# A dilated gated convolution: loads of the projection weights and of two input chunks wait until the transpose of oct 4 has landed

## Chip, cores, metric

The kernel runs on one core of a Trainium2 chip. The metric is the device time of one execution in microseconds (us); a profiled execution also gives the span from its first to its last instruction.

## The reference

A causal convolution with 15 taps and dilation 2 over x (2 x 16000 x 144, bfloat16) into 288 channels, a gate, and a projection:

```
xp = jnp.pad(x, ((0, 0), (pad, 0), (0, 0)))          # pad = 28
h = sum over i of xp[:, pad - 2*i : pad - 2*i + T, :] @ w[i]   # w: 15 x 144 x 288
z = tanh(h[..., :144]) * sigmoid(h[..., 144:])
return z @ w_o                                        # w_o: 144 x 144
```

(The sum is written here in one line; the reference loops over i.)

## The kernel before

The 32000 time steps are cut into 128 stretches of 250, one for each partition. Step e of all stretches is a tile of 128 rows; eight steps in succession are an *oct*, numbered -4 to 30, the negative ones holding the steps that the taps reach back to. TensorE needs each tile transposed (channels on partitions). Of the 144 channels, 128 go by one way and 16 by another:

- Input chunks of 16 steps (two octs) are loaded by SP's queue into `Xr` (two slots, line 500). Chunk 0 has octs 1 and 2, chunk 1 octs 3 and 4, chunk 2 octs 5 and 6, chunk 3 octs 7 and 8.
- `load_xa(o)` (line 653) copies 128 channels of an oct to `STA`, on ScalarE for octs 1 to 4 and on VectorE later, and SP issues a transposing DMA from `STA` to `XA`.
- The last 16 channels are gathered in `XBc` (lines 545, 546), differenced (646), copied to `STB` (680), and SP issues a transposing DMA to `XB` (684).
- Octs up to 0 are transposed by TensorE in the prologue (579).

The convolution is a fast algorithm: VectorE forms differences of the transposed tiles (`V`, `DU`, `DD`, `GX`, `GU`, `GV`, `GD`, line 700) and sums of the weights (630), so that a unit needs 64 matmuls (all through line 747). A pair of octs is worked in two *units* u; there are 30. A unit's items carry the names S0, S1, VE, VF, X0a to X1b, Y0a, Y0b, Y01 and D00 to D11. Among them ScalarE copies PSUM banks (905, 932, 974) and VectorE adds them: line 1026 writes into memory that was `Xp`, 1038 and 1047 add in PSUM. A D item ends four results: ScalarE takes tanh (768) and sigmoid (771), VectorE multiplies into `Z` (776). SP transposes `Z` into `ZT` (829, "ship"), TensorE multiplies by the projection weights `WOR` (846), ScalarE evicts (854), SP stores (865). Projections are the O items: up to three groups an oct of 4, 4 and 3 matmuls. The first group that is due is that of oct -1, in step 1.

`WOR` holds sixteen shifted pieces of w_o and is loaded by sixteen DMAs from GpSimd (line 1189). Every projection reads all of it.

**Order of work.** Two things set it. `PATTERNS` gives, for a step t (default `PATTERN`), the order of items in TensorE's main stream; a name with "+" belongs to unit t + 1, one without to unit t, and an item whose unit does not exist, or an O whose group is not yet due, is left out. Between them, preparation of later octs is put in, tied to the matmul it follows by `soft`. Then a planner (`_Graph.schedule`, line 113) simulates the five engines and one DMA resource with durations written in the code, and fixes from that the order of instructions on every engine and queue, and the PSUM banks. TensorE's main items keep their given order; prologue matmuls are `floating` and fill holes. On the chip each engine runs its list in order and waits on semaphores only for true dependencies (`deps`). So a new dependency acts twice: as a wait on the chip, and through a new plan.

The loads that the change touches hang on `xb2`, the transposing DMA of oct 2's `XB`: WOR's sixteen (line 1191) and the chunks from 2 on (line 1198); chunk 1 hangs on the last weight load.

Of the kernel before, what the change touches and what calls it, by code (L numbers as in the profile page):

```python
# [327 lines left out]
def _conv_wavenet_kernel(nc, x, w, w_o, out):  # L328
    B, T, D = x.shape
# [37 lines left out]
    KF = 0  # L367
    WARMS = 0
    LAG = 2
    PATTERNS = {29: 'O2 O1 Y01 Y0a D11 O0 Y0b D01 D00 D10', 28: 'Y0a X0a+ O1+ Y0b X0b+ O2+ D11 S0+ D10 X1a+ D00 Y01 S1+ X1b+ VE+ O0+ D01 VF+', 1: 'X0a+ Y0a O1+ O2+ Y0b X0b+ D11 X1a+ D00 S0+ O0+ X1b+ Y01 S1+ D10 D01 VE+ VF+', 0: 'Y0a X0a+ Y0b X0b+ D11 D00 S0+ D10 O2+ O1+ Y01 S1+ X1a+ D01 VE+ X1b+ VF+ O0+', 2: 'Y0a O0+ X0a+ O1+ Y0b X0b+ D11 D00 X1a+ S0+ D10 Y01 S1+ X1b+ D01 VE+ VF+ O2+', -1: 'X0a+ Y0a Y01 O2+ Y0b S0+ D11 D10 X0b+ O1+ X1a+ S1+ X1b+ D01 VE+ D00 O0+ VF+', 27: 'Y0a O2+ X0a+ O1+ Y0b X0b+ D11 D00 S0+ X1a+ D10 Y01 S1+ X1b+ D01 VE+ O0+ VF+'}  # L370
    AACT = (1, 2, 3, 4)
    BDVE = (3, 4)
    EARLYC = 0
# [6 lines left out]
    with contextlib.ExitStack() as st:  # L380
        def sb(name, shape, dt):
            return st.enter_context(nc.sbuf_tensor(name, shape, dt))
# [4 lines left out]
        STA = sb("STA", [NP, NST, 8, 128], BF16)  # L387
        STB = sb("STB", [NP, NST, 12, 128], BF16)
        XA = sb("XA", [NP, NA, 8, 128], BF16)
# [12 lines left out]
        WOR = sb("WOR", [NP, 16, D], BF16)  # L402
# [14 lines left out]
        x_t, w_t, wo_t, out_t = x.tensor, w.tensor, w_o.tensor, out.tensor  # L417

        g = _Graph()
# [25 lines left out]
        def aslot(o):  # L445
            return (o + 4) % NA
# [7 lines left out]
        def bslot(o):  # L454
            return (o + 1) % NB
# [20 lines left out]
        def ld_x(tile_ap, p0, p1, e0, e1):  # L476
            def f(e):
                src = bass.AP(x_t, (p0 * L - H + e0) * D, [[L * D, p1 - p0], [1, (e1 - e0) * D]])
                return e.dma_start(tile_ap, src)
            return f  # L480

        def flat(ap):
            return ap.rearrange("p e d -> p (e d)")
# [13 lines left out]
        def load_xchunk(ci):  # L497
            a, c = CH[ci]
            s = ci % NX
            return g.add("sp", ld_x(flat(Xr[:, s, 0:c - a, :]), 0, NP, E0 + a, E0 + c), w=[("Xr", s)], dur=0.5, dma="xr", nbytes=NP * (c - a) * D * 2)  # L500
# [18 lines left out]
        wa_op = wa_ops[LOADS[-1][1]] if LOADS[-1][0] == "w" else wa_ops[0]  # L519
# [50 lines left out]
        for pi in range(4):  # L570
            e0, e1 = pro_pieces[pi]
            for o in range(-4, 1):
# [3 lines left out]
                b = 6 + o % 2  # L576
# [35 lines left out]
        for o, tiles, bb in ((-1, range(E0 - 4, E0), 7), (0, range(E0, E0 + 8), 6)):  # L612
            fns = []
            for e in tiles:
# [6 lines left out]
                  r=[bk], w=[("XB", bslot(o))], frees=[bk], dur=0.5 if o < 0 else 0.92)  # L621
# [11 lines left out]
        def chunk_of(t):  # L633
            return [ci for ci, (a, c) in enumerate(CH) if a <= t < c][0]
# [6 lines left out]
        def diff_b(eng, m0, nm, r, tag):  # L641
            i0 = MB - m0 - nm

            def f(v):
                pat = lambda ph, grp: bass.AP(XBc[:].tensor, (ph * MB + i0) * DB, [[8 * MB * DB, NP], [grp, 2], [MB * DB, 2], [1, nm * DB]])
                return v.tensor_tensor(pat(2, -2 * MB * DB), pat(6, -2 * MB * DB), pat(4, 2 * MB * DB + DB), ALU.subtract)
            g.add(eng, f, r=r, w=[tag], dur=t_tt(4 * nm * DB), prio=2 if gate else 0, soft=gate[:1])

        def diff_chunk(ci):
            a, c = CH[ci]  # L650
            diff_b("dve", (E0 + a + 2) // 4, (c - a) // 4, [("XBc", ci), ("XBc", ci - 1)] if ci else [("XBc", 0)] + hk5, ("XBd", ci))

        def load_xa(o):
            s, q = aslot(o), o % NST
            ci = chunk_of(8 * o)
            i0 = 8 * o - CH[ci][0]
            src = Xr[:, ci % NX, i0:i0 + 8, 0:DA]
            if o in AACT:
                g.add("act", lambda a: a.activation(STA[:, q, :, :], src, ACT.Copy), r=[("Xr", ci % NX)], w=[("STA", q)], dur=0.92, prio=1, soft=gate[:1])  # L659
            else:  # L660
                g.add("dve", lambda v: v.tensor_copy(STA[:, q, :, :], src), r=[("Xr", ci % NX)], w=[("STA", q)], dur=0.335, prio=2, soft=gate[:1])
            g.add("sp", lambda e: e.dma_start_transpose(XA[:, s, :, :], STA[:, q, :, :].rearrange("p a b -> p (a b)")),
                  r=[("STA", q)], w=[("XA", s)], dur=1.3, dma="xa", nbytes=8 * 128 * 128 * 2)

        def load_xb(o, parts=(0, 1)):
            s, q = bslot(o), o % NST
            e0 = E0 + 8 * o
            ck = set()
            for e in range(e0 - 28, e0 + 8):
                if e >= EP:  # L670
                    ck.update([("XBc", chunk_of(e - E0)), ("XBd", chunk_of(e - E0))])
                else:
                    ck.update(hk5 + ["XBcz", "XBd_h"])
            m4 = (e0 + 2) // 4

            for h in parts:
                def cp(v, h=h):
                    src = bass.AP(XBc[:].tensor, (MB - 1 - m4 - h) * DB, [[8 * MB * DB, NP], [MB * DB, 6], [1, 128]])
                    dst = STB[:, q, 6 * h:6 * h + 6, :]
                    return v.tensor_copy(dst, src) if o in BDVE else v.activation(dst, src, ACT.Copy)  # L680
                g.add("dve" if o in BDVE else "act", cp, r=sorted(ck, key=str), w=[("STB", q, h)], dur=0.27 if o in BDVE else 0.708, prio=2 if gate else 0, soft=gate[:1])
            if 1 not in parts:
                return
            return g.add("sp", lambda e: e.dma_start_transpose(XB[:, s, :, :], STB[:, q, :, :].rearrange("p a b -> p (a b)")),
                  r=[("STB", q, 0), ("STB", q, 1)], w=[("XB", s)], dur=1.7, dma="xb", nbytes=12 * 128 * 128 * 2)
# [44 lines left out]
        def g_diffs(m, only=None):  # L730
            o0, o1, q = 2 * m + 1, 2 * m + 2, gslot(m)
            for src, sn, sl, n, dst, key, kk in ((XA, 8, aslot, 2, GX, "GX", lambda o: [("XA", aslot(o))]),
                                                 (DU, 4, uslot, 4, GU, "GU", lambda o: [("DU", uslot(o))]),
                                                 (V, 8, vslot, 2, GV, "GV", lambda o: [("V", vslot(o), 0)]),
                                                 (DD, 8, uslot, 6, GD, "GD", lambda o: [("DD", uslot(o))])):
                if only is not None and key not in only:
                    continue
                a1, am, c = sl(o1) * sn, sl(o0 - 1) * sn, sl(o0) * sn
                if n < 6:
                    tt(ap(dst, q * 2 * n, [(n, 2), n]), ap(src, a1, [(am - a1, 2), n]), ap(src, c, [(0, 2), n]),  # L740
                       kk(o1) + kk(o0) + kk(o0 - 1), [(key, q, 0), (key, q, 1)], 2 * n * TR)
                    continue
                for d, a0, ox in ((0, a1, o1), (1, am, o0 - 1)):
                    tt(ap(dst, (q * 2 + d) * n, [n]), ap(src, a0, [n]), ap(src, c, [n]), kk(ox) + kk(o0), [(key, q, d)], n * TR)
# [417 lines left out]
        xb2 = load_xb(2)  # L1162
# [19 lines left out]
        for o in range(-2, 1):  # L1182
            v_third(o)
        g_diffs(-1)
        for dl in range(8):
            for part in range(2):
                r0, r1, s0 = (16 * dl, 128, 0) if part == 0 else (0, 16 + 16 * dl, 128 - 16 * dl)
                def f(e, r0_=r0, r1_=r1, s0_=s0, i_=2 * dl + part):
                    return e.dma_start(WOR[r0_:r1_, i_, :], bass.AP(wo_t, s0_ * D, [[D, r1_ - r0_], [1, D]]))
                op = g.add("pool", f, r=["WORz"], w=[("WORp", dl, part)], dur=0.5, dma="wor", nbytes=(r1 - r0) * D * 2)  # L1190
                op.deps.add(xb2)

        nl = [1]
        nd = [1]

        def fetch(o):
            while nl[0] < len(CH) and CH[nl[0]][0] <= 8 * o:
                load_xchunk(nl[0]).deps.add(wa_op if nl[0] < 2 else xb2)
                nl[0] += 1

        def prep(o):
# [17 lines left out]
        def prepare(m):  # L1219
            o0, o1 = 2 * m + 1, 2 * m + 2  # L1220
            if m >= NPAIR:
                return []
            return [lambda: v_first(o0), lambda: v_second(o0), lambda: v_first(o1), lambda: v_second(o1), lambda: g_diffs(m, ("GX",)),
                    lambda: g_diffs(m, ("GU",)), lambda: v_third(o0), lambda: v_third(o1), lambda: g_diffs(m, ("GV",)),
                    lambda: g_diffs(m, ("GD",))]
# [7 lines left out]
        def pattern_of(t):  # L1233
            return [(x.rstrip("+"), x.count("+")) for x in PATTERNS.get(t, PATTERN).split()]

# [5 lines left out]
        for f in stage(1):  # L1241
            f()
        gate[:] = []
        for f in prepare(0):
            f()
        todo_p = []
        for t in range(-reach, NUN):
# [3 lines left out]
            for name, off in pattern_of(t):  # L1251
# [20 lines left out]
                if name[0] == "D":  # L1272
                    done_d[u] = done_d.get(u, 0) + 1
                    m, r, o0, o1 = octs(u)
# [12 lines left out]
        m, r, o0, o1 = octs(NUN - 1)  # L1287
# [89 lines left out]
```

## Time and profile before

| | us |
|---|---|
| median of 8 runs | 321.55 (320.85 to 322.27) |
| profiled execution | 321.6 |
| its span | 319.6 |
| TensorE busy | 311.9 (98%) |
| VectorE busy | 284.4 (89%) |
| ScalarE busy | 267.4 (84%) |
| granted TensorE clock | 0.997 |

In the profile's rows PE is TensorE's matmuls, PEld its weight loads, DVE VectorE, ACT ScalarE, POOL GpSimd, SP the queue that issues most DMAs ("q" marks a sequencer). A row of the timeline or of the chain begins with its start and its length in us; `xN` merges N instructions; `<-` names the tile written and those read, or in brackets what ended the wait ahead of it. A matmul's length includes its way through the array; successive ones start 0.123 us apart. A row of stretches gives the busy time of PE, PEld, DVE, ACT and POOL, the granted clock, the share of the sixteen DMA engines (over 1 where packets overlap) and GB/s. In a row of DMA issues the last number is the time from issue to landing.

### The profile page before, as it was taken

To read this page: it belongs to the slowest core of one execution; us is meant where nothing else is said; L and a number is where in the kernel's file an instruction comes from. 1 tells how busy PE (TensorE), PEld (TensorE's weight loads), DVE (VectorE), ACT (ScalarE), POOL (GpSimd) and SP (SyncE) were. 2 spreads that over 40 slices of the span, in tenths; PEclk is the share of its full clock that TensorE was granted. 3 is DMA by queue.
4 is the path that set the end of the run, shared out by engine and by line. 5 is a ranking of instruction groups with operands and counts; after the bars stand their busy time and mean duration, and the time that the engine had idled before them with its cause. 6 is when DMAs were issued, how large, how long until landed. Compare 5 with 4: busy or idle time off the path is not lost.

```text
span 319.6 us, 6912 instructions
## 1 busy us (share of the span) xinstructions
PE 311.9 (98%) x2643; PEld 239.9 (75%) x2643; DVE 284.4 (89%) x615; ACT 267.4 (84%) x635; POOL 17.0 (5%) x29
## 2 busy tenths in 40 slices
PE   7999999999999999999999999999999999999994
PEld 7677667777777777777777777777777777777674
DVE  1999999999999998998989999898989989894774
ACT  3796699899897988979798897979889797788774
POOL 8105400000000000000000000000000000000000
PEclk9999999999999999999999999999999999999998
DMA  8699959959888493979949695895949477131553
GB/s 201 206 197 173 258 108 226 171 144 178 192 159 215 93 246 83 207 157 131 251 78 238 106 201 154 146 198 121 227 118 178 104 127 188 44 71 74 113 129 94
DMA packets 127821, 50.38 MB, mean 158 GB/s; under 512 B 119134, under 2 KB 121615, under 8 KB 127789
## 3 DMA queue, kind: packets, MB, share of 16 engines
q1 hardware_dynamic: 127273, 49.62, 75.1%
q0 software_dynamic: 512, 0.33, 0.5%
q8 instruction: 20, 0.33, 0.4%
q14 instruction: 12, 0.10, 0.1%
q10 hardware_dynamic: 4, 0.01, 0.0%
HBM read 11.82 MB, written 9.22 MB: 66 GB/s over the span
## 4 chain that ended last, share of the span: by engine, by line
PE 89%; ACT 6%; DMA 2%; DVE 1%; issue 1%; POOL 0%; ACTq 0%; POOLq 0%
PE PS L747 77%; PE PS L846 9%; DMA XA<-STA 2%; ACT STB L680 2%; PE PS L554 1%; ACT STA L659 1%; PE PS L579 1%; ACT XA L588 1%; ACT XB L620 0%; ACT TS L768 0%; ACT TS L771 0%; PE PS L552 0%; PE PS L877 0%; ACT PS L905 0%; PE PS L804 0%
## 5 line engine op out<-in xcount | busy, mean ns | idle before, releaser
L1026 DVE TENSOR_TENSOR Xp<-PS,UX 128x576 f32<-128x576 f32 x90 | 63.0, 750 | 16.8 <-PE PS L747 16.6
L747 PE MATMUL PS<-WB,XB 128*128 128x288 bf16 x260 | 72.1, 286 | 0.0
L747 PE MATMUL PS<-WA,GD 128*128 128x288 bf16 x360 | 70.0, 286 | 0.1
L1038 DVE TENSOR_TENSOR PS<-PS,Xp 128x576 f32<-128x576 f32 x90 | 68.2, 758 | 2.1 <-ACT OS L854 1.0
L768 ACT ACTIVATE TS<-PS 128x288 f16<-128x288 f32 x125 | 51.7, 413 | 13.2 <-PE PS L747 12.2
L854 ACT ACTIVATE OS<-PS 128x432 bf16<-128x432 f32 (+1 forms) x88 | 42.4, 489 | 13.9 <-PE PS L846 12.8
L771 ACT ACTIVATE TS<-PS 128x288 f16<-128x288 f32 x125 | 51.4, 411 | 0.0
L905 ACT ACTIVATE PS<-PS 128x288 f32<-128x288 f32 x120 | 46.3, 408 | 2.8 <-PE PS L747 2.8
L974 ACT ACTIVATE UX<-PS 128x576 f32<-128x576 f32 x60 | 39.2, 654 | 10.7 <-PE PS L747 10.4
L680 ACT ACTIVATE STB<-XBc 128x768 bf16<-128x768 bf16 x56 | 47.5, 855 | 0.0
L747 PE MATMUL PS<-WS,GU 128*128 128x288 bf16 x210 | 44.3, 287 | 0.0
L846 PE MATMUL PS<-WOR,ZT 128*128 128x144 bf16 (+1 forms) x322 | 42.4, 253 | 0.3 <-DVE Xp L1026 0.3
L747 PEld LDWEIGHTS PS<-WA,GD 128*128 128x128 bf16 x360 | 33.7, 98 | 11.3 <-DVE PS L1038 3.1
L776 DVE TENSOR_TENSOR Z<-TS 128x288 bf16<-128x288 f16 x125 | 36.6, 298 | 4.4 <-ACT TS L771 4.2
L747 PE MATMUL PS<-WC,XB 128*128 128x288 bf16 x120 | 34.3, 286 | 0.0
L846 PEld LDWEIGHTS PS<-WOR,ZT 128*128 128x128 bf16 x322 | 27.9, 98 | 6.6 <-DVE Xp L1026 0.5
L747 PE MATMUL PS<-WD,DD 128*128 128x288 bf16 x180 | 31.9, 286 | 0.2 <-ACT PS L905 0.2
L747 PE MATMUL PS<-WC,V 128*128 128x288 bf16 x180 | 30.6, 286 | 0.0
L747 PE MATMUL PS<-WA,DD 128*128 128x288 bf16 x180 | 30.6, 286 | 0.0
L747 PEld LDWEIGHTS PS<-WB,XB 128*128 128x128 bf16 x260 | 25.4, 98 | 6.7 <-ACT XB L620 0.3
L747 PE MATMUL PS<-WA,V 128*128 128x288 bf16 x118 | 25.7, 286 | 0.3 <-ACT PS L1111 0.3
L747 PE MATMUL PS<-WT,DU 128*128 128x288 bf16 x120 | 24.5, 286 | 0.0
(93 smaller groups left out, 460.5 us busy)
## 6 DMA issues: line engine op xcount, KB each, us to landing
Xr<-in_x_dram SPq DMA_DIRECT2D x15, 576.0 KB, 4.6
out_dram<-OS SPq DMA_DIRECT2D x30, 288.0 KB, 3.1
WA<-in_w_dram SPq DMA_DIRECT2D x3, 288.0 KB, 5.8
ZT<-Z SPq DMA_TRANSPOSE x32, 3.7
Xp<-in_x_dram SPq DMA_DIRECT2D x2, 252.0 KB, 5.9
XA<-STA SPq DMA_TRANSPOSE x30, 3.5
XB<-STB SPq DMA_TRANSPOSE x30, 4.5
Xp<-in_x_dram SPq DMA_DIRECT2D x1, 441.0 KB, 4.6
```

Of the source, the lines that this page charges most:

```text
L554: fns += [lambda t: t.matmul(PS[:, BANK_O * 512:BANK_O * 512 + 128], lhsT=ID[:], rhs=ONES[:], start=True, stop=True)] * max(0, n - 12)
L680: return v.tensor_copy(dst, src) if o in BDVE else v.activation(dst, src, ACT.Copy)
L747: return lambda t: t.matmul(bank(bk.b), lhsT=lhs(), rhs=rhs(), start=start, stop=True, skip_group_check=True)
L768: return a.activation(TS[:, s, 0, :, :], both(bk, 0, D), ACT.Tanh)
L771: return a.activation(TS[:, s, 1, :, :], both(bk, D, D), ACT.Sigmoid)
L776: return v.tensor_tensor(dst, TS[:, s, 0, :, :], TS[:, s, 1, :, :], ALU.mult)
L846: return t.matmul(PS[:, c0:c0 + n * D], lhsT=ZT[:, zt, blk, :], rhs=WOR[:, wi:wi + n, :].rearrange("p a b -> p (a b)"), start=first, stop= ...
L854: return e.tensor_copy(dst, src) if eng == "dve" else e.activation(dst, src, ACT.Copy)
L905: g.add("act", lambda e: e.activation(bank(bk.b + 1), bank(bk.b), ACT.Copy), w=[bk], dur=t_act(N2), prio=0)
L974: g.add("act", lambda e: e.activation(UX[:, k, u % NU, :, :], both(X, 0, N2), ACT.Copy), r=[X], w=[("UX", k, u % NU)], frees=[X], dur=t_ac ...
L1026: g.add("dve", lambda v, k=k, wi=wi, vb=vb, us=us: v.tensor_tensor(wslot(wi), both(vb, 0, N2), UX[:, k, us, :, :], ALU.add), r=[vb, ("UX", ...
L1038: return v.tensor_tensor(both(d, 0, N2), src, wslot(wi), ALU.add)
```

## The change

Three edits. WOR's sixteen loads are added to the program later, after the staging of octs 3 and 4, and depend on the transposing DMA of oct 4 into `XA` instead of `xb2`. Chunk loads from chunk 2 on depend on that DMA too (chunks behind 3 are loaded far later anyway). The patterns of steps -1, 0, 1, 2, 28 and 29 are new, and step 3, which had the default, has one of its own; every pattern holds the same items as before.

```diff
-    PATTERNS = {29: 'O2 O1 Y01 Y0a D11 O0 Y0b D01 D00 D10', 28: 'Y0a X0a+ O1+ Y0b X0b+ O2+ D11 S0+ D10 X1a+ D00 Y01 S1+ X1b+ VE+ O0+ D01 VF+', 1: 'X0a+ Y0a O1+ O2+ Y0b X0b+ D11 X1a+ D00 S0+ O0+ X1b+ Y01 S1+ D10 D01 VE+ VF+', 0: 'Y0a X0a+ Y0b X0b+ D11 D00 S0+ D10 O2+ O1+ Y01 S1+ X1a+ D01 VE+ X1b+ VF+ O0+', 2: 'Y0a O0+ X0a+ O1+ Y0b X0b+ D11 D00 X1a+ S0+ D10 Y01 S1+ X1b+ D01 VE+ VF+ O2+', -1: 'X0a+ Y0a Y01 O2+ Y0b S0+ D11 D10 X0b+ O1+ X1a+ S1+ X1b+ D01 VE+ D00 O0+ VF+', 27: 'Y0a O2+ X0a+ O1+ Y0b X0b+ D11 D00 S0+ X1a+ D10 Y01 S1+ X1b+ D01 VE+ O0+ VF+'}
+    PATTERNS = {29: 'O1 O0 O2 Y0a D11 Y01 Y0b D01 D00 D10', 28: 'Y0a X0a+ O0+ Y0b X0b+ D11 S0+ O1+ D00 D10 X1a+ Y01 S1+ X1b+ VE+ D01 O2+ VF+', 1: 'X0a+ Y0a X0b+ Y0b D11 O0+ O2+ D00 X1a+ S0+ Y01 X1b+ S1+ D10 D01 VE+ VF+ O1+', 0: 'Y0a X0a+ O2+ Y0b X0b+ O1+ D11 S0+ D00 D10 S1+ X1a+ O0+ Y01 VE+ X1b+ D01 VF+', 2: 'O1+ Y0a X0a+ O0+ Y0b X0b+ D11 D00 X1a+ S0+ D10 Y01 S1+ X1b+ D01 VE+ VF+ O2+', -1: 'Y0a Y0b O2+ Y01 D10 D11 X0a+ S0+ O0+ X0b+ X1a+ S1+ D00 O1+ D01 X1b+ VE+ VF+', 27: 'Y0a O2+ X0a+ O1+ Y0b X0b+ D11 D00 S0+ X1a+ D10 Y01 S1+ X1b+ D01 VE+ O0+ VF+', 3: 'Y0a X0a+ O2+ O1+ Y0b D11 X0b+ D00 S0+ X1a+ D10 Y01 S1+ X1b+ D01 VE+ VF+ O0+'}
...
+        land = {}
+
         def load_xa(o):
...
-            g.add("sp", lambda e: e.dma_start_transpose(XA[:, s, :, :], STA[:, q, :, :].rearrange("p a b -> p (a b)")),
+            land[o] = g.add("sp", lambda e: e.dma_start_transpose(XA[:, s, :, :], STA[:, q, :, :].rearrange("p a b -> p (a b)")),
...
-        for dl in range(8):
-            for part in range(2):
...
-                op = g.add("pool", f, r=["WORz"], w=[("WORp", dl, part)], dur=0.5, dma="wor", nbytes=(r1 - r0) * D * 2)
-                op.deps.add(xb2)
-
...
-                load_xchunk(nl[0]).deps.add(wa_op if nl[0] < 2 else xb2)
+                load_xchunk(nl[0]).deps.add(wa_op if nl[0] < 2 else land.get(4, xb2))
...
         for f in stage(1):
             f()
         gate[:] = []
+        for dl in range(8):
+            for part in range(2):
...
+                op = g.add("pool", f, r=["WORz"], w=[("WORp", dl, part)], dur=0.5, dma="wor", nbytes=(r1 - r0) * D * 2)
+                op.deps.add(land[4])
+
```

More of the change, by code (lines that the diff above doesn't have):

```diff
@@ L1184, in _conv_wavenet_kernel @@
         g_diffs(-1)
-        for dl in range(8):
-            for part in range(2):
-                r0, r1, s0 = (16 * dl, 128, 0) if part == 0 else (0, 16 + 16 * dl, 128 - 16 * dl)
-                def f(e, r0_=r0, r1_=r1, s0_=s0, i_=2 * dl + part):
-                    return e.dma_start(WOR[r0_:r1_, i_, :], bass.AP(wo_t, s0_ * D, [[D, r1_ - r0_], [1, D]]))
-                op = g.add("pool", f, r=["WORz"], w=[("WORp", dl, part)], dur=0.5, dma="wor", nbytes=(r1 - r0) * D * 2)
-                op.deps.add(xb2)
         nl = [1]
@@ L1243, in _conv_wavenet_kernel, with f @@
         gate[:] = []
+        for dl in range(8):
+            for part in range(2):
+                r0, r1, s0 = (16 * dl, 128, 0) if part == 0 else (0, 16 + 16 * dl, 128 - 16 * dl)
+                def f(e, r0_=r0, r1_=r1, s0_=s0, i_=2 * dl + part):
+                    return e.dma_start(WOR[r0_:r1_, i_, :], bass.AP(wo_t, s0_ * D, [[D, r1_ - r0_], [1, D]]))
+                op = g.add("pool", f, r=["WORz"], w=[("WORp", dl, part)], dur=0.5, dma="wor", nbytes=(r1 - r0) * D * 2)
+                op.deps.add(land[4])
         for f in prepare(0):
```

## The prediction

> **What bounds the kernel now.** I read the page's first and fourth parts first: which engine is busy, and what the chain that ended last consists of.
>
> ```profile
> PE 311.9 (98%) x2643; PEld 239.9 (75%) x2643; DVE 284.4 (89%) x615; ACT 267.4 (84%) x635; POOL 17.0 (5%) x29
> PE 89%; ACT 6%; DMA 2%; DVE 1%; issue 1%; POOL 0%; ACTq 0%; POOLq 0%
> ```
>
> TensorE sets the time; the other 11% lies at the two ends. The chain in order of time says where:
>
> ```profile
> 28.64 5.93 DMA XA<-STA
> 34.60 0.76 DVE V L700 x2
> 35.36 0.69 DVE PS L1038
> 36.09 2.68 PE PS L747 x20
> ...
> 62.83 7.89 PE PS L747 x64
> ```
>
> From 53 us on a unit is 64 convolution matmuls in 7.9 us (0.123 us each) with eleven projection matmuls after them, and nothing can be taken out there by moving loads. The transpose of oct 4 (issued 28.64, landed 34.57) is the only DMA in the chain after 28 us. Next I asked what stands around it: the transposes and loads on SP, WOR's sixteen loads on GpSimd, and landing times.
>
> ```profile
> 27.09 1.51 SPq L684 DMA_TRANSPOSE XB<-STB  x1
> 28.64 1.83 SPq L662 DMA_TRANSPOSE XA<-STA  x1
> 30.51 2.76 SPq L684 DMA_TRANSPOSE XB<-STB  x1
> 33.32 1.06 SPq L479 DMA_DIRECT2D Xr<-in_x_dram  x2
> ```
> ```profile
> 27.42 8.50 POOL L1189 DMA_DIRECT2D WOR<-in_w_o_dram  x16 [14.57 <-DMA XB<-STB]
> ```
> ```profile
> XA<-STA SPq DMA_TRANSPOSE x30, 3.5
> DMA to landing us min/median/max: 4.0/4.6/5.8
> WOR<-in_w_o_dram POOLq DMA_DIRECT2D x1, 36.0 KB, 5.3
> ```
>
> The first landing row is the median of all XA transposes, the second WOR's sixteen loads, the third WOR's last load: issued 35.34, landed 40.6. Oct 4 took 5.93 us where 3.5 is usual, and WOR's loads run beside it. But the two loads of chunks 2 and 3 are not in its way: SP issues them at 33.32, because it is still issuing XB until 33.27. So of the two things held back, only WOR moves.
>
> How tight is what waits? VectorE around the landing, the busy time by stretch (PE, PEld, DVE first), and TensorE's own rows:
>
> ```profile
> 33.78 0.77 DVE L1047 TENSOR_TENSOR PS<-PS,UX 128x576 f32<-128x576 f32 x1
> 34.60 0.76 DVE L700 TENSOR_TENSOR V<-XA 128x512 bf16<-128x512 bf16 x2
> ```
> ```profile
> 30.00:35.00 5.00, 5.00 (x43) 3.98 (x42) 4.88 (x10) 2.12 (x5) 5.00 (x11) 1.00 1.26 205
> 40.00:45.00 5.00, 4.74 (x40) 3.49 (x38) 4.89 (x12) 4.42 (x10) 0.00 (x0) 1.00 0.39 79
> ```
> ```profile
> 42.32 0.41 PE L747 MATMUL PS<-WV,V 128*128 128x288 bf16 x2
> 42.99 0.41 PE L846 MATMUL PS<-WOR,ZT 128*128 128x144 bf16 x3 [0.26 <-DVE Xp L1026]
> ...
> 46.53 0.29 PE L747 MATMUL PS<-WB,XB 128*128 128x288 bf16 x1
> 47.00 0.42 PE L747 MATMUL PS<-WT,XA 128*128 128x288 bf16 x2 [0.18 <-ACT TS L771]
> ```
>
> VectorE ends L1047 at 34.55 and takes up oct 4's V at 34.60: it waited 0.05 us for the landing. It is busy 4.88 to 5.00 us of every 5 from 25 to 55 us. The long transpose is in the chain, but VectorE is full behind it. TensorE's losses, start to start less 0.123 us a matmul: 0.26 before 36.09, 0.18 and 0.10 before 38.78 and 39.13, 0.42 before 42.99, 0.12 before 45.66, 0.35 before 47.00; together 1.43 us. That is all the ramp from 25 to 50 us holds.
>
> **The change part by part.** The profiled execution took 321.6 us at a span of 319.6, so 2.0 us lie around the span; it stands 0.05 us over the median of 321.55. Sums go by the span.
>
> *Oct 4 lands earlier.* The XA transpose before it (issued 23.98, behind an XB, with no WOR load beside it) took 4.1 us, the median is 3.5, its own time is 5.93. So its landing L is at 32.1, 32.7 or 34.6; I take 32.7, the row most like it (SP still has the 5.8 us XB of 27.09 ahead). Worth: directly the 0.05 us of VectorE's wait; at best also the 0.26 us gap at 36.09, if V is then run before L1047 instead of just ahead of L1038. VectorE has no hole to put it in, so I take -0.1 between 0 and -0.26.
>
> *Chunks 2 and 3 wait for L.* On SP, behind the waiting load, stand its twin, ZT of oct 0 (36.27) and XA of oct 5 (40.60). The wait begins at 33.3, so it is 0 at L = 32.7 and 1.3 us at L = 34.6. Chunk 2 landed at 38.0 and VectorE first touches it at 40.02; chunk 3 landed at 40.1 and is touched at 41.66. Slack 2.0 and 1.5 us cover even 1.3: cost 0. Were the cover gone, VectorE, which runs in order, would lose what exceeds it. Should the planner put these loads ahead of oct 4's XB, that XB waits too, at most from 30.5 to L, for a first use at 43.8, 6.8 us after it landed at 37.0: 0.
>
> *WOR's sixteen loads wait for L.* Nothing else is on GpSimd after 12.9 us, so nothing is queued behind them there. The waiter is TensorE: a projection needs all sixteen. Before, the first issue came 0.3 us after its releaser, the last 7.92 us after the first. The last lands at W = L + 0.3 + 7.92 + 4.6 = 45.5, with the median landing. The ends: 32.1 + 8.22 + 4.0 = 44.3, and 34.6 + 8.22 + 5.3 = 48.1. The median fits better than the last load's 5.3, because that one ran beside both 576 KB loads, which now come ahead of it.
>
> The Trainium skill prices a load from GpSimd otherwise (DMA: Bandwidth & Descriptors, "Anatomy of one DMA"): about 2.0 us plus bytes over 436 GB/s, which makes 2.1 us for 36 KB, W = 43.0 and by that sum no wait here at all. This trace disagrees: the shortest of the sixteen took 4.0 us.
>
> *The first projection moves.* Before, it stands third in unit 1's pattern; in the new one it comes after Y0b, X0b and D11, 4 + 6 + 8 = 18 matmuls later. Unit 1 starts at 42.08; 22 matmuls from there end at P = 44.8 if D11 waits for nothing. If D11 still waits for L1047 (ended 44.42 before), P = 44.45 + 8 x 0.123 = 45.4. I take 45.1. WOR's slack was 1.9 us (TensorE was through at 42.32 + 2 x 0.123 = 42.57, the last load down at 40.64); it becomes P - W = -0.4, with ends +1.1 and -3.3. So TensorE, whose main order is fixed and has no filler left, stands still 0.4 us, between 0 and 3.3. In exchange the 0.42 us bank wait at 42.99 goes, but what is late next is L1047 in the full VectorE: I take -0.1 of it. A stop at 45 lets VectorE and ScalarE catch up, so it swallows the gaps at 45.66 and 47.00 (0.47 us): net 0 for a stop of 0.4.
>
> *The replanned rest.* The units before 0 run the same items in the same order; in unit 0 D01 falls behind X1b. In the last unit six projection groups stand in front instead of four, and Y01 goes behind D11, so L1038 for D01 starts at about 309.5 instead of 307.74 and D01 at 310.3 instead of 309.87: +0.4 us unless hidden. The opposite bound is the 0.40 us wait at 297.86 disappearing. I take 0 between -0.4 and +0.4.
>
> Sum: -0.1 - 0.1 + 0 + 0 = -0.2: span 319.4, time 321.4.
>
> **Rivals.** About 0.2% (0.64 us) is what a measurement of this kernel can tell from no change; the forecast case stays inside it.
>
> *Slower: the first projection waits for WOR.* It decides once W passes P by the 0.47 us that is swallowed plus 0.64, thus at W over 46.2, which needs L over 33.4 or slow landings. For it: XB of 27.09 took 5.8 us itself and its data go ahead of oct 4's in the same queue; WOR's 0.33 MB take 0.5% of the DMA engines' span (the page's third part), 1.6 us of all sixteen spread over 13, so they may not be what stretched oct 4. With L = 34.6 and a median landing W = 47.4, a stop of 2.3, net +1.8, less the 0.2 above: 323.2. Against it: the DMA share was 1.26 in 30 to 35 us with WOR in it, the highest of the ramp. The Trainium skill's rule is on this side (DMA: Bandwidth & Descriptors, "Rules for kernel authors"): issue a DMA early and wait on its semaphore late; the row of 1.9 us slack before shows the early issue paying.
>
> *Faster: the ramp closes.* If W is before P and VectorE's order comes out better, up to all 1.43 us go, and half to all of it gives 320.2 to 320.9; say 320.5. Against it: VectorE is full and the amount of its work does not change.
>
> *It does nothing:* chunks 2 and 3 were never early, and WOR is only a small share. Then 321.55, within the forecast's band.
>
> **How the numbers follow.** Forecast with the do-nothing case 0.42; WOR late 0.30; ramp closes 0.28. The likeliest alone runs from 320.9 to 322.2. The range reaches into both rivals, to 320.1 (all of the ramp) and 323.2 (WOR at L = 34.6), leaving about 0.1 outside on each side. Faster 0.28, same 0.42, slower 0.30.
>
> **What would show it.** Right: the XA transpose of oct 4 lands in about 4 us; WOR's first issue right after it and its last landing near 45.5; the first L846 row shortly after that, with a gap of under 1 us and no gap near 47; VectorE still full to 55 us; 7.9 us per 64 matmuls later. Wrong: oct 4 still takes over 5.5 us, or the first L846 row starts after 46.5 with WOR's DMA as its releaser (slower), or TensorE's rows from 25 to 50 us show no gaps (faster), or the last 20 us changed by more than 0.5 us.

## The result and the profile after

The changed kernel takes 323.91 us (median of 19 runs, 322.71 to 325.58) where the one before takes 321.72 (54 runs): a ratio of 1.0064 with a 95% interval of 1.0051 to 1.0077. By the ratio that is 2.06 us more; the two medians differ by 2.19. The profiled execution took 323.38 us at a span of 321.7, against 321.6 and 319.6.

The first and fourth parts of the page of the changed kernel:

```profile
PE 311.7 (97%) x2643; PEld 239.5 (74%) x2643; DVE 284.3 (88%) x615; ACT 267.9 (83%) x635; POOL 17.0 (5%) x29
...
PE 87%; ACT 7%; DMA 3%; SPq 1%; issue 1%; DVE 0%
```

Every engine does the same work in the same time (TensorE 311.7 us after 311.9); the 2.1 us between the spans are added idle time. SP's sequencer and the GpSimd row of the changed kernel (start, length, what is issued, in brackets the wait before it):

```profile
27.20 1.51 SPq L686 DMA_TRANSPOSE XB<-STB  x1
28.76 1.91 SPq L664 DMA_TRANSPOSE XA<-STA  x1
30.71 1.53 SPq L686 DMA_TRANSPOSE XB<-STB  x1
33.36 0.80 SPq L479 DMA_DIRECT2D Xr<-in_x_dram  x2
36.54 1.30 SPq L831 DMA_TRANSPOSE ZT<-Z  x1
41.34 1.43 SPq L686 DMA_TRANSPOSE XB<-STB  x1
42.82 3.75 SPq L664 DMA_TRANSPOSE XA<-STA  x2
```
```profile
33.65 8.87 POOL L1242 DMA_DIRECT2D WOR<-in_w_o_dram  x16 [20.66 <-DMA XA<-STA]
```

Oct 4's transpose (28.76) landed at 33.35. Chunks 2 and 3 go out at 33.36, where they went out before (33.32). WOR's loads start at 33.65 instead of 27.42, and the sixteenth is issued at 41.94. The DMA issues of the changed kernel, by the time from issue to landing, oct 4's `XA` first, WOR's sixteenth load last:

```profile
XA<-STA SPq DMA_TRANSPOSE x1, 4.6
...
WOR<-in_w_o_dram POOLq DMA_DIRECT2D x1, 36.0 KB, 5.0
```

So oct 4 is 1.3 us quicker (4.59 after 5.93 us), and WOR is complete at 41.94 + 5.01 = 46.95. Now the chain of waits of the changed kernel, in order of time, around that point and at a unit of the steady part:

```profile
43.55 2.39 PE PS L749 x18
45.96 0.41 ACT TS L770
46.37 0.31 ACT TS L773
46.68 0.36 issue
47.04 0.41 PE PS L848 x3
47.45 0.75 PE PS L749 x6
48.22 0.41 ACT TS L770
48.63 0.31 ACT TS L773
48.99 4.64 PE PS L749 x36
...
139.79 7.89 PE PS L749 x64
```

and TensorE's own rows:

```profile
43.55 0.42 PE L749 MATMUL PS<-WS,GU 128*128 128x288 bf16 x2 [0.44 <-ACT PS L907]
...
45.64 0.29 PE L749 MATMUL PS<-WC,XB 128*128 128x288 bf16 x1
47.04 0.41 PE L848 MATMUL PS<-WOR,ZT 128*128 128x144 bf16 x3 [1.12 <-ACT TS L773]
...
48.99 0.42 PE L749 MATMUL PS<-WD,DD 128*128 128x288 bf16 x2 [0.31 <-ACT TS L773]
```

The first projection should follow the matmul of 45.64 at 45.76; it starts at 47.04, a stop of 1.28 us. The row names ScalarE's sigmoid (L773) as releaser, but that ended at 46.68; the chain admits it by "issue 0.36", time for which it found no cause. The cause is WOR's last load at 46.95, 0.09 us before the matmul. Here the named engine had long been done and the true releaser is a DMA: in e1, f5, h2 and i1 below, which keep this order and have WOR down earlier, the stop is gone.

The 64 matmuls of a steady unit still take 7.89 us. The rest of the loss is small change: start to start less 0.123 us a matmul, TensorE's gaps from 25 to 75 us sum to 1.99 us before and 3.68 after. That is 1.28 for the stop and 0.41 in several places (36 to 40 us: 0.56 became 0.65; at 43: 0.52 became 0.60; 45.6 to 49.3: 0.50 became 0.52; 52 to 75: 0.40 became 0.62). The prologue is 0.30 us longer in this profile (its end, the matmul of 24.61, stood at 24.31 before); h1, the same kernel profiled again, has 24.23.

From the steady unit to the end of the span it is 181.87 us after 181.82. That hides two changes which nearly cancel. First the chain of the changed kernel, then that of the kernel before, at the end:

```profile
308.29 3.96 DMA ZT<-Z
...
312.29 0.68 PE PS L879 x8
...
317.75 0.44 PE PS L806 x4
```
```profile
315.38 0.42 PE PS L804 x4
```

Counted from the steady unit, TensorE's last matmul ends 0.76 us later (178.74 us after it, 177.98 before): in the last unit TensorE now waits for a transpose of `Z`, among others. The last store, issued 0.76 us later too, then landed in 2.17 us instead of 2.88 and gave 0.71 us back.

### The profile page after: what moved, and what is told of

Read it like the earlier page. It is cut to its first block, busy times and chain, and to the rows that moved or that the text cites. A ratio compares the mean times of both kernels' runs of the same rounds, so it can differ in the third digit from the quotient of the medians.

```text
span 321.7 us, 6911 instructions
## 1 busy us (share of the span) xinstructions
PE 311.7 (97%) x2643; PEld 239.5 (74%) x2643; DVE 284.3 (88%) x615; ACT 267.9 (83%) x635; POOL 17.0 (5%) x29
## 4 chain that ended last, share of the span: by engine, by line
PE 87%; ACT 7%; DMA 3%; SPq 1%; issue 1%; DVE 0%
PE PS L749 78%; PE PS L848 9%; DMA Xp<-in_x_dram 2%; ACT STB L682 1%; DMA ZT<-Z 1%; ACT TS L770 1%; ACT TS L773 1%; ACT STA L661 1%; SPq L479 1%; ACT OS L810 0%; ACT PS L907 0%; ACT XB L620 0%; SPq L491 0%; PE PS L579 0%; ACT XA L588 0%
## 5 line engine op out<-in xcount | busy, mean ns | idle before, releaser
L773 ACT ACTIVATE TS<-PS 128x288 f16<-128x288 f32 x125 | 51.3, 411 | 0.0
L907 ACT ACTIVATE PS<-PS 128x288 f32<-128x288 f32 x120 | 45.9, 406 | 2.8 <-PE PS L749 2.8
L749 PEld LDWEIGHTS PS<-WS,GU 128*128 128x128 bf16 x210 | 18.6, 98 | 8.6 <-ACT PS L907 1.4
```

The source lines that it names most:

```text
L749: return lambda t: t.matmul(bank(bk.b), lhsT=lhs(), rhs=rhs(), start=start, stop=True, skip_group_check=True)
L773: return a.activation(TS[:, s, 1, :, :], both(bk, D, D), ACT.Sigmoid)
L907: g.add("act", lambda e: e.activation(bank(bk.b + 1), bank(bk.b), ACT.Copy), w=[bk], dur=t_act(N2), prio=0)
```

## The experiments

**How they are read.** Two things vary in any profile: the prologue (the first matmul after its last gap, at 24.31 us before, lies between 23.2 and 24.6), and the landing of the last store (2.9 us after its issue before, 2.2 in the changed kernel, 4.8 in f2 and f4). A span alone therefore misleads by 1 to 2 us. I use the *ramp*, from that first matmul to the start of the steady unit: 137.81 - 24.31 = 113.50 us before, 139.79 - 24.61 = 115.18 after. Ratios are to the kernel before on the same chip, in five rounds of runs.

Theories: **A**, the first projection waits for WOR; **B**, the loss comes from the new patterns and the new plan that comes with them; **C**, it comes from the held chunks.

A new dependency also replans everything. To part the two, most kernels add or drop the dependency *after* the planner's call, so that all engines keep their order and only one wait differs. "Old plan" is the order of the kernel before, "new plan" that of the changed one. In old-plan kernels `land` is filled as in the change.

| kernel | ratio [95%] | ramp, less 113.50 | oct 4, issue to landing | stop at the first projection |
|---|---|---|---|---|
| changed | 1.0064 [1.0051, 1.0077] | +1.68 | 4.6 | 1.28 |
| h1, changed again | 1.0058 [1.0031, 1.0085] | +2.0 | 4.7 | 1.59 |
| e1, new plan, WOR early | 1.0033 [1.0016, 1.0051] | +1.56 | 6.2 | 0 |
| e2, old plan, WOR late | 1.0025 [1.0007, 1.0043] | +0.82 | 4.8 | 1.71 |
| e3, old plan, chunks late | 0.9993 [0.9979, 1.0008] | +0.1 | 6.2 | as before |
| e4, new patterns alone | 1.0035 [1.0014, 1.0056] | +1.2 | 5.3 | 0.11 |
| f1, holds, old patterns | 1.0074 [1.0048, 1.0099] | +2.5 | 5.0 | 2.45 |
| f4, old plan, WOR at 13 us | 1.0007 [0.9986, 1.0028] | +0.2 | 4.8 | as before |
| f5, new plan, WOR at 13 us | 1.0037 [1.0015, 1.0058] | +0.75 | 4.8 | 0 |
| h2, new plan, half early | 1.0045 [1.0024, 1.0066] | +1.4 | 6.1 | 0 |
| i1, new plan, split | 1.0011 [0.9997, 1.0024] | +0.40 | 4.9 | 0 |
| i2, old plan, split | 0.9987 [0.9975, 0.9999] | -0.21 | 4.8 | as before |

**e1: the changed kernel's plan, with WOR's wait put back to `xb2`.**

```diff
-        _ms = g.schedule()
+        _ms = g.schedule(); [(op.deps.discard(land[4]), op.deps.add(xb2)) for op in g.ops if op.dma == "wor"]
```

> The changed kernel with its whole plan (the order on every engine and queue) kept, and one wait put back: WOR's first load waits for the XB transpose of oct 2 again instead of the XA transpose of oct 4. Theory A (WOR wait): the 2.2 us are TensorE's stop at the first projection (1.28 us at 47.0) and what follows from it; without the stop 321.7 to 322.4, no gap before the first L848 row, WOR's last load down at about 41, XA of oct 4 landing near 34.9 again (6 us) with next to no cost. Theory B (new plan): the loss lies in the new order on TensorE, VectorE and ScalarE; then 323.3 to 323.9, with gaps of 0.5 us or more left between 37 and 50 us.

Measured: 322.50 us against 321.76. The stop is gone, and only about half the loss with it. The trace says why; VectorE, then TensorE, of e1:

```profile
34.48 0.42 DVE L702 TENSOR_TENSOR V<-XA 128x512 bf16<-128x512 bf16 x1 [1.03 <-DMA XA<-STA]
34.82 0.76 DVE L1049 TENSOR_TENSOR PS<-PS,UX 128x576 f32<-128x576 f32 x1
```
```profile
35.64 0.54 PE L749 MATMUL PS<-WA,DD 128*128 128x288 bf16 x3 [0.84 <-DVE PS L1049]
```

The new plan puts half of oct 4's `V` ahead of L1049. With WOR beside it, oct 4 took 6.2 us, VectorE stood still for 1.03 us and TensorE for 1.00. One stop has been exchanged for another: the new plan needs the early oct 4 that the hold buys.

**e2: the old plan, with WOR alone held.**

```diff
+        _ms = g.schedule(); [op.deps.add(land[4]) for op in g.ops if op.dma == "wor"]
```

> The kernel before with its whole plan kept and one wait moved: WOR's first load waits for the XA transpose of oct 4. Theory A: WOR's last load lands at about 46.7 (33.2 + 0.3 + 8.3 + 5.0) where TensorE reaches the first projection at 42.6, so a stop of some 4 us; nothing swallowed gives 325.7, 0.5 us of later gaps swallowed gives 325.2. Theory B: the wait itself is nearly hidden, at most 322.4.

Measured: 322.46 against 321.76. TensorE of e2, where the releaser is named rightly:

```profile
42.01 0.41 PE L747 MATMUL PS<-WV,V 128*128 128x288 bf16 x2
43.96 0.41 PE L846 MATMUL PS<-WOR,ZT 128*128 128x144 bf16 x3 [1.54 <-DMA WOR<-in_w_o_dram]
```

The expected stop of some 4 us did not come: WOR's last load, issued at 41.38, landed in 2.5 us and not in 5.0, at 43.87. The hold by itself, with no pattern changed, costs a 1.71 us stop, and the ramp grows by only 0.82: the stop covers the 0.63 us of gaps that stood at 42.99, 43.33 and 45.66, and the one at 36.09 shrinks from 0.26 to 0.05, since oct 4 took 4.8 us. A alone is a part of the loss, not all.

**e3: the old plan, with chunks 2 and 3 held.**

```diff
+        _ms = g.schedule(); [op.deps.add(land[4]) for op in [op for op in g.ops if op.dma == "xr"][2:]]
```

> The kernel before with its whole plan kept and one wait added: the load of chunk 2 waits for the XA transpose of oct 4, chunk 3 behind it in the queue. All theories that I hold: 321.7 (within 0.5): SP comes to this load at 33.3, the transpose lands at 34.6, and the chunk's slack to its first use is 2.0 us. A rival: VectorE, which is full, comes to it late and the time grows by the 1.3 us of the wait, 323.0.

Measured: 321.40 against 321.76, no difference. The hold did bind: oct 4 landed at 33.99 and the two chunks went out at 34.01, 0.9 us after SP had finished the issue before them. C falls.

**e4: the kernel before with the new `PATTERNS`, nothing held, planned anew.**

> The kernel before with only the new PATTERNS, the loads hanging on the XB transpose of oct 2 as before; the planner plans anew. Theory A: no stop for WOR, so within 0.6 us of 321.7. Theory B: the patterns cost what was lost, 323.3 to 323.9.

Measured: 322.45 against 321.76. The patterns without the hold lose 1.2 us of ramp. So B is not nothing; but e1 and e4 both run these patterns with a late oct 4 (6.2 and 5.3 us), which is not what they meet in the changed kernel.

**f1: both holds with the old `PATTERNS`, planned anew.**

> The changed kernel with the old PATTERNS, planned anew with both holds. Theory D (two costs that add up: new patterns some 1.1 us, WOR's late landing some 0.8 us): only the second is left, 322.3 to 322.8, a stop of 1 to 2 us at the first projection. Theory A alone (all is the WOR wait): as bad as the changed kernel or worse, since the first projection stands earlier, 323.9 or more.

Measured: 324.48 against 321.98. TensorE of f1:

```profile
44.76 0.42 PE L848 MATMUL PS<-WOR,ZT 128*128 128x144 bf16 x3 [2.29 <-DMA WOR<-in_w_o_dram]
```

A stop of 2.45 us. This is the outcome that was expected if the wait for WOR were all; without the new patterns the loss is not smaller. The new patterns do what their order suggests: with the projection moved back by 18 matmuls the stop is 1.28 to 1.59 instead of 2.45. It does not fall by all of the 2.2 us of 18 matmuls, since WOR was down earlier in f1: its last load landed in 3.1 us after 5.0.

**f2, f3, f6: the kernel before with some of the new patterns, planned anew**: step 1 alone; steps -1 and 0; steps 2 and 3.

> The kernel before with the new pattern of step 1 alone (first projection behind D11, X0b ahead of Y0b), planned anew, loads as before. If step 1 carries the 1.1 us of the new patterns: 322.5 to 322.9, with the gap of 0.5 to 0.6 us ahead of X0b's WS,GU rows and one near 46 to 49. If the others (steps -1, 0, 2, 3) carry it: 321.5 to 322.0.

> The kernel before with the new patterns of steps -1 and 0 alone, planned anew, loads as before. If the new patterns' cost lies here: 322.5 to 322.9, with gaps of 0.2 to 0.3 us each before unit 0's Y01 and VE (38 to 40 us). If it is spread over the steps, as the rows of the changed kernel's plan without the stop suggest (0.26 us here, 0.2 at step 1, 0.3 at steps 2 and 3): 321.9 to 322.1.

> The kernel before with the new patterns of steps 2 and 3 alone, planned anew, loads as before. Spread theory: gaps of 0.2 and 0.07 us at 62 to 64 us that the old plan does not have, 321.9 to 322.0. If the cost lies here: 322.5 or more. If the re-searched patterns are no worse: 321.7.

Measured: 0.9999 [0.9978, 1.0020], 1.0005 [0.9987, 1.0024] and 1.0005 [0.9987, 1.0023]; the ramps grew by 0.8 (0.46 of it from an oct 4 that took 6.6 us), 0.4 and 0.6 us. None of them singly carries e4's loss beyond the interval; these runs did not settle which pattern the ramp's loss comes from. The new patterns of steps 28 and 29 were not run alone, but the traces show their part: from the steady unit to the end of the last matmul it is 178.74 to 178.78 us in all seven kernels that have them, 177.98 to 178.03 in the nine that don't. In six of the seven the last store landed 2.17 to 2.18 us after its issue, in six of the nine 2.88 to 2.90, so about 0.7 of the 0.76 us came back there. Whether it does in executions without a profile was not measured.

**f4, f5: WOR's sixteen loads hang on the last weight load `wa_op`, at about 13 us**, in the old and the new plan.

```diff
+        _ms = g.schedule(); [(op.deps.discard(xb2), op.deps.add(wa_op)) for op in g.ops if op.dma == "wor"]
```

(f5 discards `land[4]` instead.)

> The kernel before with its plan kept; WOR's loads wait for the last weight load (13.7 us) instead of the XB transpose of oct 2 (27.1). All sixteen then land by about 27, clear of oct 4's transpose and of the first projection. Theory: XA of oct 4 lands about 4.7 us after its issue, the gap at 36 us falls from 0.26 to about 0.05, time 321.5 (-0.2). Rival: WOR's packets stretch the transposes of octs 1 and 2 in their place, TensorE waits between 15 and 30 us, 322.5.

> The changed kernel with its plan kept; WOR's loads wait for the last weight load instead of the XA transpose of oct 4, so neither the stop at the first projection nor WOR traffic beside oct 4's transpose is left. Theory D: 1.28 us of stop less and VectorE's wait for oct 4 stays short: 322.3 to 322.7, the rest being the new patterns. If the new plan were good once its loads are right: 321.7 or less.

Measured: 321.67 and 323.03 against 321.98. Both get the quick oct 4 (4.8 us) and no stop for WOR, but VectorE of f4 shows the new price:

```profile
25.18 0.63 DVE L680 COPY STB<-XBc 128x768 bf16<-128x768 bf16 x2 [0.38 <-DMA XB<-STB]
```

Sixteen loads from 13.4 to 21.9 us lie beside the transpose of oct 1's `XB`, which took 5.54 us from issue to landing (5.33 in f5) instead of 3.95 and landed at 25.16; TensorE lost 0.38 (0.35) us at 27. The collision was moved to an earlier transpose.

**h1, h2: the changed kernel once more, and its plan with the first eight loads on `xb2`, the last eight on `land[4]`.**

```diff
+        _ms = g.schedule(); [(op.deps.discard(land[4]), op.deps.add(xb2)) for op in [op for op in g.ops if op.dma == "wor"][:8]]
```

> The changed kernel once more, beside the next one. How steady are the landing of oct 4 (33.3 in the first profile), of WOR's last load (46.95, 5.0 us after its issue) and the stop (1.28 us)? If W hangs on L and on sixteen issues of 0.53 us, the last issue comes 8.3 us after the first again and the stop is 0.5 to 1.5 us; 323.5 to 324.1.

> The changed kernel with its plan kept; the first eight of WOR's loads wait for the XB transpose of oct 2 as before the change, only the last eight for the XA transpose of oct 4. If the issue time on GpSimd makes WOR late (0.53 us a load), the last load is issued 4.2 us sooner and lands by about 42, ahead of the first projection: no stop, 322.5 to 323.0, the new patterns' cost alone. If the stop has another cause (the projection's bank, ZT, the order on VectorE), it stays: 323.7.

Measured: 323.48 and 323.11 against 321.71. h1 repeats the result, with a stop of 1.59 us (last load issued 42.07, landed 46.89). In h2 the stop is gone, but eight loads at 27 us are enough to stretch oct 4 to 6.1 us, and TensorE loses 0.87 us at 34.93 as in e1.

**i1, i2: the loads split, eight at `wa_op`, eight at `land[4]`**, in the new and the old plan: out of the way of oct 1's `XB`, of oct 4's `XA`, and of the projection.

```diff
+        _ms = g.schedule(); [(op.deps.discard(land[4]), op.deps.add(wa_op)) for op in [op for op in g.ops if op.dma == "wor"][:8]]
```

(i2: `op.deps.discard(xb2)` for all, then `wa_op if i < 8 else land[4]`.)

> The changed kernel with its plan kept; eight of WOR's loads wait for the last weight load (13.7 us), the last eight for the XA transpose of oct 4 as changed. Neither the stop at the first projection is left (last load down by about 41) nor WOR traffic beside oct 4's transpose. What remains against the kernel before is the new patterns by themselves. If the changed kernel's rows are read rightly (1.28 us stop, 0.4 us other gaps, 0.1 in the last units): 322.2 to 322.5. If the new patterns carry half of the loss (1.1 us): 322.8.

> The same split on the kernel before, its plan kept: eight loads of WOR at 13.7 us, eight after oct 4's transpose. The intent of the change without its price: oct 4 lands in about 4.7 us, the gap at 36 us falls to about 0.05, WOR is down by about 41, 1.5 us ahead of the first projection: 321.2 to 321.5 (0.2 to 0.5 less than before). If the early eight stretch the XB transpose of oct 1: a new gap near 27 us and 321.7.

Measured: 321.82 and 321.15 against 321.37. GpSimd, then TensorE, of i1:

```profile
13.77 4.33 POOL L1242 DMA_DIRECT2D WOR<-in_w_o_dram  x8 [1.57 <-DMA WA<-in_w_dram]
33.22 4.19 POOL L1242 DMA_DIRECT2D WOR<-in_w_o_dram  x8 [15.12 <-DMA XA<-STA]
```
```profile
44.90 0.29 PE L749 MATMUL PS<-WC,XB 128*128 128x288 bf16 x1
45.03 0.41 PE L848 MATMUL PS<-WOR,ZT 128*128 128x144 bf16 x3
...
46.98 0.42 PE L749 MATMUL PS<-WD,DD 128*128 128x288 bf16 x2 [0.26 <-ACT TS L773]
```

The projection follows at once, 0.123 us after the matmul before it. The eight early loads do stretch oct 1's `XA` (4.2 us from issue to landing, 3.2 before), and TensorE does not wait for it. Otherwise i1's gaps are those of the changed kernel one by one, to 0.06 us: the ramp is 1.28 us shorter, which is the stop and nothing else. The ratio falls from 1.0064 to 1.0011. That is A shown by itself: the stop is 1.3 to 1.6 us by the traces and about 1.7 by the ratios. What is left in i1, 0.40 us of ramp, and the last unit's 0.76 us of which the last store gives 0.71 back, is B: the new patterns and plan, once oct 4 is early. The interval of i1's ratio includes 1, so that i1 is slower at all is not shown by its times.

In i2 the old plan gets the early oct 4 for nothing. TensorE of i2 around the gap that was 0.26 us at 36.09:

```profile
35.83 0.29 PE L747 MATMUL PS<-WC,XB 128*128 128x288 bf16 x1
36.01 0.42 PE L747 MATMUL PS<-WA,GD 128*128 128x288 bf16 x2
```

0.05 us is left of it, and the kernel is at 0.9987 [0.9975, 0.9999], the only one of these that beats the kernel before, and by little: one of twelve intervals in the table missing 1 by 0.0001 can be chance. That the gap shrinks is surer, since e2 shows the same 0.05. The hold's idea is worth about 0.2 us of ramp here; its form, all sixteen loads behind one landing, costs several times that.

## Why the prediction was wrong

The forecast was 321.4 with a range to 323.2; it is 323.91, slower and above the range. The mechanism is that of the rival "the first projection waits for WOR", whose point of decision (W over 46.2) held: W was 46.95. Two steps failed: the stop, put at 0.4 us, was 1.28 (W and P below), and the gaps that it was to swallow stayed. By the rival's own sum a stop of 1.28 gives only 322.2 (0.47 swallowed, 0.2 gained elsewhere), so the stop alone does not carry the time over the range.

- **Oct 4 lands earlier, and WOR is what stretched it.** Right. Eight profiles with no WOR load beside the transpose show 4.6 to 5.0 us, eight with WOR (the kernel before among them) 5.3 to 6.6; e2 moved nothing but the sixteen loads and has 4.8. So the doubt raised under the rival, that 0.5% of the DMA engines' span cannot stretch a transpose, was wrong. L was put at 32.7 and was 33.35: half a microsecond because the new duration is 4.6 and not the 4.1 of the row it was taken from, the rest because oct 4 was issued later. (That row did have WOR's first loads beside its last 0.7 us, against what the prediction says; without them it is 4.14 in the changed kernel, so nothing hangs on it.) The -0.1 for it was not seen: the gap of 0.26 at 36.09 went, but under the new order others grew, and the gaps from 36 to 40 us went from 0.56 to 0.65 in all.
- **Chunks 2 and 3: 0.** Right (e3, and issue times of 33.32 and 33.36).
- **W, WOR's last landing: 45.5 put, 46.95 measured.** The 0.3 us from releaser to first issue was exact. L gave 0.65 of the miss; fifteen issues took 8.29 instead of 7.92 us, 0.37; the landing took 5.01 instead of 4.6, 0.41. L and the landing lay within the bounds given for them, the issue time had been given none, and all three erred to the same side.
- **P, when TensorE is ready: 45.1 put, 45.76 measured**, 0.30 of it the prologue of this profile. With W - P at 1.19 the stop is 1.28 instead of 0.4.
- **"A stop at 45 ... swallows the gaps at 45.66 and 47.00 (0.47 us): net 0 for a stop of 0.4."** This step failed. VectorE and ScalarE did catch up (busy time by stretch of the changed kernel; PE, PEld, DVE, ACT, POOL):

```profile
40.00:45.00 5.00, 4.56 (x38) 3.44 (x36) 4.95 (x11) 5.00 (x10) 2.52 (x5) 1.00 0.63 127
45.00:50.00 5.00, 3.57 (x29) 2.33 (x28) 3.95 (x10) 3.04 (x9) 0.00 (x0) 1.00 1.28 176
```

  VectorE falls to 3.95 us of 5 and ScalarE to 3.04, and TensorE still waits 0.48 and 0.05 us at 48.99 and 49.29, where it waited 0.34 and 0.05 at 47.00 and 47.30 before. The chain above shows why: six matmuls after the stop (47.45) feed the tanh (48.22) and the sigmoid (48.63), and these free the next matmul (48.99). The gap is a round trip that begins *behind* the stop; engines that have caught up ahead of it can't shorten it. i1, without the stop, has the gap at 0.42. The gap at 45.66 did go, but in i1 it is gone as well: the new order removed it, not the stop. (The prediction's list of gaps, 1.43 us, also leaves out 0.10 at 43.33 and 0.05 at 47.30.) In e2 the stop did swallow 0.63 us, two gaps at its own place and one behind it, while the one before the `XA` matmuls (47.67 there) stayed. In these two kernels a stop swallows the waits whose producers can go on during it, no others.
- **"I take -0.1" for the bank wait at 42.99.** It went, as said, but the first matmul of X0b now waits for L907 at 43.55: 0.60 us in place of 0.52.
- **The replanned rest: 0 between -0.4 and +0.4.** Measured +0.22 between 52 and 75 us. In the last unit D01 began 0.95 us later against the steady unit (312.80, before 309.87), where 0.4 had been put as the upper bound, and TensorE ended 0.76 us later. That only 0.05 us of it reached the span is the last store's quicker landing, which the prediction did not foresee: here the sum was saved by luck. The 0.40 us wait at 297.86 stayed (299.84).

Added up for the two profiles: 0.09 + 0.08 + 0.02 + 1.28 + 0.22 to 75 us, 0.05 behind it, 0.30 of prologue, 2.0 in all, the difference of the spans (321.66 and 319.63 before rounding). The prologue is chance, so the trace accounts for 1.7 of the 2.06 us that the ratio gives; h1's trace, with its stop of 1.59, for 2.1. How long the stop is in executions without a profile was not measured.

The Trainium skill (DMA: Bandwidth & Descriptors, "Rules for kernel authors") says to issue a DMA early and to wait on it late. The runs agree: with the first eight issues moved ahead, nothing else, the stop of 1.28 us is 0 in i1. The same page's price for a load from GpSimd ("Anatomy of one DMA": about 2.0 us plus bytes over 436 GB/s, an estimate of 2.1 us for 36 KB) is met nearly in e2, where the last load took 2.5 us, and missed in the changed kernel, with 5.0. In the changed kernel the loads of 9 and 31.5 KB issued at 40.03 and 40.53 took 1.96 and 1.98 us, about that price. So it holds here for a load at a quiet time, and says little of one issued beside the transposes.

## What to carry to other kernels

When a group of loads is held back, its cost is set by the *last* of the group, and the issue time of all of them stands between the release and that one: sixteen small loads at 0.53 us each are 8 us before the last is even issued. Subtract a later gap from a new stop only if what the gap waits for is already under way ahead of the stop. And to keep small loads off a critical transfer, split them over two quiet places rather than push all behind it; then look at which other transfer lies in the place they were moved to. When orders at both ends of a kernel are changed together, look at both: a span can stay the same because two changes cancel.

## What the runs showed of the hardware

- Sixteen loads of 4.5 to 36 KB, 0.33 MB in all, stretch a transpose that runs beside them: oct 4's `XA` takes 5.3 to 6.6 us from issue to landing instead of 4.6 to 5.0, and oct 1's `XB` 5.54 instead of 3.95 (f4). Eight of the loads do it as well (`XA` 6.1 in h2).
- GpSimd issues a load every 0.53 us in the quiet case, but single issues took 0.87 us (the changed kernel, at 41.07), 1.11 us (f1, at 38.93) and 1.20 us (h1, at 40.39). I don't know why.
- The same 36 KB load took 2.5 us in e2 and 5.0 in the changed kernel. In the longer case SP had issued an `XB` transpose 0.60 us ahead of it (41.34), and the two landed within 0.24 us of each other; in h1 the two landed 0.22 us apart. In e2 an `XA` transpose had gone ahead, and both landed within 0.20 us too, early. That the small load ends with the transpose ahead of it is a reading of these traces, not an experiment.
- The last of the three stores that end the kernel landed 2.17 us after its issue where it came 1.5 us behind the one ahead of it (the changed kernel), 2.88 us where it came 0.8 us behind (the kernel before). That the distance is the reason was not tested.
